# Four attention layers with exponentials on two engines: one step of VectorE's exponential and the token normalization go to GpSimd, and an unmasked pair of head groups is selected ahead

## The chip, the cores and the metric

The kernel runs on one core of a Trainium2 chip. The metric is device time in microseconds, lower is better. Before the change the median of three runs was 2004.07 us (2001.56 to 2004.95).

## The reference

Four layers work on x of 2048 tokens by 512 features, in bfloat16, with 32 heads of 16 features: A, B, A, B, with a layer norm ahead of each and a residual sum behind it. In the kernel they are layers 0, 1, 2 and 3. Layers 0 and 2 share weights, and so do 1 and 3.

```python
# A: four segments of 512 tokens, one after the other
logits = einsum('bhqd,bhkd->bhqk', qs, ks) * scale + mask     # mask is causal, inside the segment
a_dot = einsum('bhqk,bhkd->bhqd', softmax(logits), vs)
a_mem = (phi(qs) @ M) / (phi(qs) @ z + 1e-06)                  # memory of the segments before
o = g * a_mem + (1.0 - g) * a_dot                              # g = sigmoid(beta), one per head
M = M + phi(ks)^T vs;  z = z + sum(phi(ks))
# B: full attention over all 2048 tokens
p = softmax(einsum('bhqd,bhkd->bhqk', q, k) * Dh ** (-0.5))
o = einsum('bhqk,bhkd->bhqd', p, v)
```

Each layer ends with a projection by wo. The bulk of the work is the exponential of the scores: two layers of 32 heads x 2048 x 2048 unmasked, and two of 32 heads x 4 segments with the masked half of 512 x 512 left out where a whole block of it is masked.

## The kernel before

**A program written by a planner.** Python code builds the instruction lists of all engines in one pass. It keeps an estimated clock per engine (Sched, line 76) and chooses, step by step, what to issue next, so constants and estimated durations (`ns=`) decide the order of the instructions. On the chip each engine runs its own list in order, with semaphore waits where data or buffers are needed.

**Banks and units.** The scores are computed transposed, a bank at a time: 128 keys by 512 queries of one head, a 32-row matmul of K by a masked copy of Q (qm, made in line 1159, on GpSimd or on VectorE). Eight heads with one c and one parity e share a qm tile and make up groups: an A group e=0 has 12 banks and its mate 8; a B group has 16 banks for each key segment, 64 in all where all four are there. Two groups (e = 0, 1) are a pair. A unit is three banks in one half of PSUM's banks 0 to 5: TensorE fills them, one ScalarE activation of 128x1536 (line 1244) makes the exponentials, pT, and TensorE multiplies pT by V (with a column of ones for the denominators) into bank 6. Masked banks get their triangle cut by GpSimd (line 1259) in between. When a group is done, `finish` divides bank 6 by its denominators on VectorE: reciprocal (line 1312), for an A group a product with 1 - g (line 1318), and the product that makes the output tile ob (line 1324). A transposing DMA of SyncE brings ob to oT.

**Exponentials on VectorE.** `dx_pick` may take a bank of a selected B group away from ScalarE, at most one a unit. It is computed into bank 7, and VectorE evaluates the exponential by arithmetic. Line 910 evacuates the bank as a fixed-point number into dxt, KA, or QA (the names of tiles are reused as space); two banks make a chain of 1024 columns: line 936 forms z from the low half of the number, line 939 squares z, line 941 multiplies by a constant and adds another, line 943 squares again, line 945 joins the high half and writes the result dxo, which TensorE multiplies by V like any pT. Two chains (`task_dx` 0 and 1) can be under way. A group gives at most a fifth (TAKEN = 5) of its 64 banks, 12. The state is called wide once layer 0 is complete: there are then four input buffers, and one output slot more, in space that layer 0 needed.

**What sets the order.** `select` keeps a list of selected groups: it takes the next pair of A groups if its K and Q are ready, else of B groups, when at most one group is left (or two short B groups). It gives B pairs back that have not begun when an A pair of layer 2 becomes ready. Projections, layer norms, the memory of layers 0 and 2, and output projections are generator tasks; each step names what it needs, its matmuls and its VectorE time, and `background` and `bg_one` run steps as credits (CR_A in units of A groups, CR_W in wide units) and the estimated lateness of VectorE against TensorE (EARLY, DVE_LATE, DX_LATE) allow. Projections use bank 7 too. `keep_busy` adds matmuls of zeros where the planner expects TensorE to be too idle (FILL).

The layers overlap: layer 2's segments can begin once layer 1 has handed over their tokens, so four stretches of A groups of layer 2 lie between B groups of layer 1. The order in the trace is layer 0 with the first short B groups up to about 375 us; then B groups of layer 1 with the A groups of layer 2 at about 525, 771, 1017 and 1210 us; and layer 3's B groups from about 1258 us to the end.

Layer norms: for each tile of 128 tokens, statistics on VectorE (lines 511, 513), then line 538 subtracts the mean and multiplies by the reciprocal deviation, 512 columns in bfloat16, into one of two xn tiles. A transposing DMA makes xT from it.

Of the kernel before, what the change touches and what calls it, by code (L numbers as in the profile page):

```python
# [3 lines left out]
dt = mybir.dt  # L4
# [252 lines left out]
class Builder:  # L257
    NPU = 4
    WARM, WARM2 = 84, 20
    LAG_A = 2  # L260
    NDX = 4
# [12 lines left out]
    DMA_STEPS, DMA_LATE = 2, 300  # L274
# [9 lines left out]
    def alloc(self):  # L284
# [23 lines left out]
        self.qm = sb("qm", [P, 4, 512], bf)  # L308
# [10 lines left out]
        self.gout = sb("gout", [P, H], f32)  # L319
        self.M = sb("M", [P, NCH, 8, 17], f32)  # L320
# [32 lines left out]
        self.b_qm = n1("qm", 4)  # L353
# [7 lines left out]
        self.b_bet, self.b_g, self.b_gout = B("bet"), B("g"), B("gout")  # L361
        self.b_M, self.b_Mn, self.b_Mz = n1("M", 2), B("Mn"), B("Mz")
# [135 lines left out]


# [33 lines left out]
    def normalize(self, s, k, i):  # L533
        t = 4 * s + i
        n = self.ring("xn", 2)
        xn = self.xn[:, n, :]
        mean, rstd = self.lnst[:, k, i, 6:7], self.lnw[:, k, 1, i:i + 1]
        self.op("dve", lambda e: e.tensor_scalar(xn, self.x[:, t, :], mean, rstd, op0=ALU.subtract, op1=ALU.mult),
                reads=[self.b_x[t], self.b_lnst[k][i], self.b_lnw[k]], writes=[self.b_xn[n]], ns=410)
        return n, xn, self.b_xn[n]  # L540
# [213 lines left out]
    def task_out(self, L, s):  # L754
        isA = L % 2 == 0
        wo, bwo = (self.woA, self.b_woA) if isA else (self.woB, self.b_woB)
        for ti in range(4):
# [3 lines left out]
            if isA and s > 0 and ti == 0:  # L761
                for c in range(NCH):
                    yield [("dma", ("oT", L, s, c)), ("dma", ("amemT", L, s, c))], 0, 450
                    o, m = self.oT[:, 0, c, :], self.phq[:, c, :]
                    self.op("dve", (lambda o, m: lambda e: e.tensor_tensor(o, o, m, ALU.add))(o, m),
                            reads=[self.b_phq[c], self.b_oT[0][c]], writes=[self.b_oT[0][c]], ns=420)
                need.append(self.later())
# [70 lines left out]
    def dx_pick(self, items):  # L838
# [8 lines left out]
        for n, g in enumerate(self.sel):  # L847
            rest += len(g.banks) - g.pos
            if g.kind != "B" or g.total < 64 and self.near < 150 or g.shut or g.taken >= g.total // (self.TAKEN if self.wide else 6) or rest < (self.REST if self.wide else 30):
                continue  # L850
# [62 lines left out]

    def dx_close(self):
        self.dx_pairs.append((self.dx_bufs.pop(0), self.dx_build))
        self.dx_build = []

    def task_dx(self, k):
        while True:
# [3 lines left out]
            yield from self.dx_chain(k, b, ents, self.dx_free.pop(0))  # L923

    def dx_chain(self, k, b, ents, slot):
# [6 lines left out]
        out = self.dx_space("out", slot)  # L932
        z, ob = self.dx_space("z", k)[:, 0:w], out.bitcast(dt.int16)[:, 0:w]
        bt, bo, bz = self.b_dxt[b], [self.b_dxo[slot]], [self.b_dxz[k]]
# [6 lines left out]
        self.op("dve", lambda e: e.tensor_scalar(z, z, EXP_B, EXP_A, op0=ALU.mult, op1=ALU.add), reads=bz, writes=bz, ns=ns[1])  # L941
# [49 lines left out]
    def met(self, need):  # L991
# [4 lines left out]
        def ok(n):  # L996
# [6 lines left out]
            if n == "pair":  # L1003
                return len(self.dx_pairs) > 0 and len(self.dx_free) > 0
# [128 lines left out]
    def select(self, late):  # L1133
        tail = self.sel[-2:]
        if len(self.sel) > 2 and self.seqA and self.seqA[0][0].L and all(g.kind == "B" and not g.pos for g in tail) and self.met(self.group_needs(self.seqA[0][0])):
# [5 lines left out]
        while len(self.qm_free) > 1 and (len(self.sel) <= 1 or len(self.sel) == 2 and all(g.kind == "B" and g.total < 64 for g in self.sel)):  # L1141
            pair = None
            for seq in (self.seqA, self.seqB):
                if seq and self.met(self.group_needs(seq[0][0])):
                    pair = seq.pop(0)
                    break
# [4 lines left out]
            for g in pair:  # L1151
# [9 lines left out]
                self.sel.append(g)  # L1161
# [129 lines left out]
    def finish(self, g):  # L1291
# [21 lines left out]
        if g.kind == "A":  # L1313
            assert self.b_gout.last_write is not None and self.step > 2
            h = 8 * g.c + g.e
            om = bcast(self.gout[:, h:h + 1], [[0, 4], [2, 4]])
            r4 = rd.rearrange("p (t r) -> p t r", r=4)
            self.op("dve", lambda e: e.tensor_tensor(r4, r4, om, ALU.mult), reads=[br, self.b_gout], writes=[br], ns=160)  # L1318
        if g.e == 0:
            self.oi = self.ring("ob", 2)  # L1320
        oi = self.oi
# [8 lines left out]
    def run_deferred(self, now):  # L1330
        while self.deferred and (now or self.deferred[0][0] <= self.step):
            _, g, oi = self.deferred.pop(0)
            own = self.oT_owner.get((g.L % 2, g.c))
            if own is not None:
                while ("op",) + own not in self.flags:
                    self.bg_must(own)
            self.oT_owner[(g.L % 2, g.c)] = (g.L, g.qseg)
# [5 lines left out]
    def pv_taken(self, g, now, used=()):  # L1343

        for ent in [t for t in self.dxq if t[1] is g and (now or t[0] <= self.step)]:
            _, _, what, r, slot, i = ent
            if r in used:
                continue
            self.dxq.remove(ent)
            self.pv(g, what, r, self.dx_space("out", slot)[:, 512 * i:512 * i + 512], self.b_dxo[slot])  # L1350
            used = tuple(used) + (r,) if not now else ()
# [149 lines left out]
```

## Time and profile before

| what | value |
|---|---|
| median of three runs | 2004.07 us |
| the profiled execution, whole | 2004.62 us |
| its span, first to last instruction | 2002.9 us |
| mean granted TensorE clock | 0.988 |
| activations of line 1244 (three banks each) | 1413, 1712 ns each |
| banks that VectorE evacuates (line 910) | 249 + 125 + 123 = 497 |
| chains of 1024 columns, of 512 | 239, 19 |
| GpSimd's qm (line 1159), masks (line 1259) | 86.0 us, 176.6 us |
| line 1318 on VectorE | 64 times, 176 ns median |
| line 538 on VectorE | 60 times, 408 ns median |

The duration of an instruction overlaps with the next one on its engine, so durations add up to more than the time: 1413 activations of 1712 ns are 2419 us, but their union is 1912 us. What an instruction costs its engine is the spacing from start to start. An engine's busy time is the union. GpSimd's duration includes time in which it has begun and can't go on.

### The profile page before, as it was taken

Reading aid. Unit: us, or ns where it says so; the run is one execution under the profiler, and the core shown is the slowest. Engines: PE = TensorE matmul, PEld = TensorE weight load, DVE = VectorE, ACT = ScalarE, POOL = GpSimd, SP = SyncE. Lnnn points to the kernel's source line nnn. Section 1 sums busy time; section 2 is a strip of 40 time slices with the busy share of each in tenths; the row PEclk is TensorE's granted clock in tenths of the full one; section 3 lists DMA queues with packets and bytes.
Section 4 is the critical chain, followed back from the end, with each engine's and each line's share of the span. In section 5 each row is a group of like instructions: output and inputs, shape, how many; then the busy total and the mean of one; then the engine's idle time right before and its main releaser. Section 6 shows DMA issues by size and latency. Waiting matters only on the chain.

```text
span 2002.9 us, 61442 instructions
## 1 busy us (share of the span) xinstructions
PE 1721.0 (86%) x27135; PEld 890.5 (44%) x27135; DVE 1631.9 (81%) x2979; ACT 1942.2 (97%) x1456; POOL 270.5 (14%) x450
## 2 busy tenths in 40 slices
PE   7888888888878888888888888888888888888888
PEld 4444444444444444444444444444444444444443
DVE  5665555599779895899948996469999999999997
ACT  7899999999999999999999999999999999999998
POOL 3422223110220003100031004101000000000000
PEclk9999999999999999999999999999999999999999
DMA  5111111000100000000011001100000000000000
GB/s 154 33 28 18 31 28 25 4 10 15 18 10 15 5 15 20 18 15 5 15 20 18 5 17 24 20 4 7 15 5 5 5 15 5 5 5 15 5 7 12
DMA packets 100939, 34.76 MB, mean 17 GB/s; under 512 B 93504, under 2 KB 100160, under 8 KB 100672
## 3 DMA queue, kind: packets, MB, share of 16 engines
q1 hardware_dynamic: 100672, 30.83, 8.0%
q8 instruction: 212, 3.47, 0.8%
q14 instruction: 55, 0.45, 0.1%
HBM read 6.30 MB, written 2.10 MB: 4 GB/s over the span
## 4 chain that ended last, share of the span: by engine, by line
ACT 58%; issue 19%; PE 9%; DVE 6%; DMA 1%; POOL 1%; SPq 0%; ACTq 0%; DVEq 0%
ACT pT L1244 57%; PE ps L393 9%; POOL pT L1259 1%; DVE ob L1324 1%; DMA phq<-amem 1%; DVE dxt L910 1%; DVE dxo L945 1%; ACT amem L602 0%; DVE rd L1312 0%; DVE rd L1318 0%; DVE qm L1159 0%; DVE dxz L936 0%; DVE amem L691 0%; DVE KA L910 0%; DVE dxz L939 0%
## 5 line engine op out<-in xcount | busy, mean ns | idle before, releaser
L1244 ACT ACTIVATE pT<-ps 128x1536 bf16<-128x1536 f32 x1413 | 1912.4, 1712 | 43.1 <-PE ps L393 36.0
L393 PE MATMUL ps<-qm,KB 32*128 32x512 bf16 x4096 | 508.8, 386 | 192.9 <-ACT pT L1244 167.0
L393 PE MATMUL ps<-VB,pT 128*128 128x51 bf16 (+1 forms) x14396 | 578.6, 186 | 14.4 <-DVE ob L1324 6.5
L393 PEld LDWEIGHTS ps<-VB,pT 128*128 128x128 bf16 x14396 | 459.6, 96 | 294.5 <-issue 223.5
L393 PEld LDWEIGHTS ps<-qm,KB 32*128 32x128 bf16 x4096 | 130.9, 91 | 525.6 <-ACT pT L1244 487.9
L393 PE MATMUL ps<-wB,zero 128*128 128x512 bf16 x1121 | 357.9, 381 | 0.0
L1259 POOL TENSOR_SCALAR_AFFINE_SELECT pT<-pT 128x768 bf16<-128x768 bf16 (+4 forms) x320 | 176.6, 567 | 510.4 <-ACT pT L1244 509.1
L1159 POOL TENSOR_SCALAR qm<-QB,par 128x512 bf16<-128x512 bf16 x86 | 86.0, 1003 | 1117.2 <-PE ps L393 1097.3
L910 DVE TENSOR_SCALAR dxt<-ps 128x512 uint32<-128x512 f32 x249 | 170.9, 687 | 16.4 <-PE ps L393 14.5
L393 PE MATMUL ps<-VA,pT 128*128 128x51 bf16 (+1 forms) x2560 | 110.5, 190 | 34.6 <-DVE ob L1324 22.8
L393 PEld LDWEIGHTS ps<-VA,pT 128*128 128x128 bf16 x2560 | 85.0, 98 | 77.2 <-POOL pT L1259 37.0
L393 PE MATMUL ps<-qm,KA 32*128 32x128 bf16 (+2 forms) x1536 | 88.7, 260 | 21.8 <-ACT pT L1244 15.1
L393 PE MATMUL ps<-VB,dxo 128*128 128x51 bf16 (+1 forms) x1596 | 104.7, 185 | 0.3 <-DVE dxo L945 0.2
L910 DVE TENSOR_SCALAR KA<-ps 128x512 uint32<-128x512 f32 x125 | 85.7, 686 | 4.6 <-PE ps L393 3.5
L910 DVE TENSOR_SCALAR QA<-ps 128x512 uint32<-128x512 f32 x123 | 84.4, 686 | 5.5 <-PE ps L393 4.9
L939 DVE TENSOR_TENSOR dxz<-dxz 128x1024 f16<-128x1024 f16 (+1 forms) x129 | 86.9, 673 | 0.7
L943 DVE TENSOR_TENSOR dxz<-dxz 128x1024 f16<-128x1024 f16 (+1 forms) x129 | 86.5, 670 | 0.5
L939 DVE TENSOR_TENSOR VA<-VA 128x1024 f16<-128x1024 f16 (+1 forms) x129 | 86.4, 670 | 0.6
L943 DVE TENSOR_TENSOR VA<-VA 128x1024 f16<-128x1024 f16 (+1 forms) x129 | 85.4, 662 | 0.6
L393 PEld LDWEIGHTS ps<-qm,KA 32*128 32x128 bf16 x1536 | 39.1, 93 | 92.6 <-ACT pT L1244 42.3
L393 PEld LDWEIGHTS ps<-wB,zero 128*128 128x128 bf16 x1121 | 78.4, 96 | 0.0
L393 PE MATMUL ps<-xT,wA 128*128 128x512 bf16 x256 | 69.2, 388 | 1.3 <-DVE amem L691 0.4
(124 smaller groups left out, 1601.2 us busy)
## 6 DMA issues: line engine op xcount, KB each, us to landing
out_dram<-x SPq DMA_DIRECT2D x8, 256.0 KB, 2.1
x<-in_A_x_dram SPq DMA_DIRECT2D x3, 512.0 KB, 8.7
wB<-in_B_wqkv_dram SPq DMA_DIRECT2D x1, 1536.0 KB, 12.7
oT<-ob SPq DMA_TRANSPOSE x63, 2.4
xT<-xn SPq DMA_TRANSPOSE x60, 2.5
x<-in_A_x_dram SPq DMA_DIRECT2D x4, 128.0 KB, 2.2
wA<-in_A_wk_dram SPq DMA_DIRECT2D x1, 512.0 KB, 4.3
wA<-in_A_wq_dram SPq DMA_DIRECT2D x1, 512.0 KB, 5.3
```

The lines of the kernel that those rows point to most:

```text
L393: self.sc.add("pe", lambda e: e.matmul(out, lhsT, rhs, start=start, stop=stop, skip_group_check=True), reads=reads, banks=[(bank, "w", all ...
L910: self.op("dve", lambda e: e.tensor_scalar(d, o, SCALE * LOG2E * 65536, 126.0 * 65536, op0=ALU.mult, op1=ALU.add), writes=self.dx_writes(" ...
L939: self.op("dve", lambda e: e.tensor_tensor(z, z, z, ALU.mult), reads=bz, writes=bz, ns=ns[0])
L943: self.op("dve", lambda e: e.tensor_tensor(z, z, z, ALU.mult), reads=bz, writes=bz, ns=ns[0])
L945: self.op("dve", lambda e: e.scalar_tensor_tensor(ob, hi, 128.0, z, op0=ALU.mult, op1=ALU.add), reads=bt + bz, writes=self.dx_writes("out" ...
L1159: self.op(eng, (lambda m, q, col: lambda e: e.tensor_scalar(m, q, col, 0.0, op0=ALU.mult, op1=ALU.add))(m, q, col), reads=[bq, self.b_par] ...
L1244: self.sc.add("act", (lambda dst, src: lambda e: e.activation(dst, src, ACT.Exp, scale=SCALE))(dst, src), writes=self.b_pT[slot * 3 + i:sl ...
L1259: self.op("pool", (lambda blk, pat: lambda e: e.affine_select(blk, blk, pattern=pat, compare_op=ALU.is_ge, fill=0.0, base=0, channel_multi ...
L1324: self.op("dve", lambda e: e.tensor_tensor(ob, src[:, :, 0:16], rb, ALU.mult), reads=[br] + bsrc, writes=[self.b_ob[oi][g.e]], bank=bk, al ...
```

## The change

1. In `dx_chain`, the product and sum of line 941 go from VectorE to GpSimd where the state is wide and no A group is selected (`masks()`). The planner counts it as 1350 ns of GpSimd. The second square (line 943) is ordered only where the planner expects GpSimd to be done (`("done", o)`). The output slot is taken ahead of line 945 and no longer at the chain's start; there are three slots (NDX) instead of four, and one more when wide.
2. `normalize` may put line 538 on GpSimd, with no A group selected and GpSimd's estimated clock behind.
3. `select`: when wide, a full B pair is selected behind A groups, and A pairs that become ready are put in ahead of a B pair that has not begun, in place of the giving back. Six qm tiles instead of four. `dx_pick` can then take banks of that B pair while A groups run.
4. The factor 1 - g leaves `finish` (line 1318 goes). It is applied to oT, per partition, from a small tile gfm: with the sum of the memory's part in one instruction (24 times, in place of line 765's sum), and by itself in segment 0 (8 times).
5. `pv_taken` does at most one product of a taken bank a step (PV_TAKEN) in place of one a row group not in use, and `run_deferred` waits for an output projection instead of forcing it.
6. Constants of the planner: among them EARLY 400 to 200, FILL 0.58 to 0.62, CR_A 1150 to 1450, CARRY and CARRY_W 0 to 400 and 800, ALT3 2 to 1, GAP 3 to 2, PE_B and PE_A one up, DVE_LATE 1500 to 1200, DX_FIN 2500 to 9000, PAIRS2 1 to 0.

```diff
+    XN_POOL = 1
+    POOL_T = 1350
+    LOOK, PV_TAKEN = 1, 1
+    NQM = 6
-    NDX = 4
+    NDX = 3
-    EARLY = 400
-    FILL = 0.58
+    EARLY = 200
+    FILL = 0.62
-    DVE_FIN, DX_FIN = 600, 2500
+    DVE_FIN, DX_FIN = 600, 9000
-    DX_BANK, DX_LATE, BG_BANK, DVE_LATE, DVE_LATE_LOW = 500, 3000, 200, 1500, 3500
-    CR_A, CR_B, CR_W, CR_LOW, CARRY, CARRY_W, REST, NEAR, SLACK = 1150, 1500, 1700, 2600, 0, 0, 36, 30, 300
-    ALT3, ALT5, GAP, AHEAD, PE_B, PE_A, PE_LOW, LOW, PAIRS, TAKEN, PAIRS2 = 2, 4, 3, 250, 3, 2, 5, 24, 30, 5, 1
+    DX_BANK, DX_LATE, BG_BANK, DVE_LATE, DVE_LATE_LOW = 500, 3000, 200, 1200, 5000
+    CR_A, CR_B, CR_W, CR_LOW, CARRY, CARRY_W, REST, NEAR, SLACK = 1450, 1500, 1700, 2600, 400, 800, 36, 30, 300
+    ALT3, ALT5, GAP, AHEAD, PE_B, PE_A, PE_LOW, LOW, PAIRS, TAKEN, PAIRS2 = 1, 4, 2, 250, 4, 3, 5, 24, 30, 5, 0
...
+        pool = self.XN_POOL and not self.masks() and self.sc.t["pool"] < max(self.sc.t["dve"], self.sc.t["pe"])
+        self.op("pool" if pool else "dve", lambda e: e.tensor_scalar(xn, self.x[:, t, :], mean, rstd, op0=ALU.subtract, op1=ALU.mult),
...
-            if isA and s > 0 and ti == 0:
+            if isA and ti == 0:
...
+                    if s == 0:
+                        yield [("dma", ("oT", L, s, c))], 0, 360
+                        self.op("dve", (lambda o, gc: lambda e: e.tensor_scalar(o, o, gc, 0.0, op0=ALU.mult, op1=ALU.add))(o, gc),
...
+                    self.op("dve", (lambda o, m, gc: lambda e: e.scalar_tensor_tensor(o, o, gc, m, op0=ALU.mult, op1=ALU.add))(o, m, gc),
...
+    def masks(self):
+        return any(g.kind == "A" for g in self.sel)
...
-        self.op("dve", lambda e: e.tensor_scalar(z, z, EXP_B, EXP_A, op0=ALU.mult, op1=ALU.add), reads=bz, writes=bz, ns=ns[1])
-        yield [], 0, c[1]
+        o = self.op("pool" if self.POOL_T and self.wide and not self.masks() else "dve", lambda e: e.tensor_scalar(z, z, EXP_B, EXP_A, op0=ALU.mult, op1=ALU.add),
...
+        yield [("done", o)], 0, c[1]
         self.op("dve", lambda e: e.tensor_tensor(z, z, z, ALU.mult), reads=bz, writes=bz, ns=ns[0])
-        yield [], 0, c[2]
+        yield ["slot"], 0, c[2]
+        slot = self.dx_free.pop(0)
...
+            if n[0] == "done":
+                return self.bubble or self.forcing or n[1].eng == "dve" or n[1].end < max(self.sc.t["dve"], self.sc.t["pe"]) + 60
...
+            look = self.LOOK and self.wide
+            at = next((i for i, g in enumerate(self.sel) if g.kind == "B" and g.e == 0 and not g.pos), len(self.sel)) if look else len(self.sel)
+            few = at <= 1 or not look and at == 2 and all(g.kind == "B" and g.total < 64 for g in self.sel)
+            short = look and len(self.sel) == 2 and all(g.kind == "B" and g.total < 64 for g in self.sel)
+            if self.seqA and (few or short) and self.met(self.group_needs(self.seqA[0][0])):
+                pair = self.seqA.pop(0)
...
+            elif self.seqB and at == len(self.sel) and (few or short or look and self.seqB[0][0].total == 64 and all(g.kind == "A" for g in self.sel)) and self.met(self.group_needs(self.seqB[0][0])):
+                pair = self.seqB.pop(0)
...
-                self.sel.append(g)
+                self.sel.insert(at + i, g)
...
-        if g.kind == "A":
...
-            self.op("dve", lambda e: e.tensor_tensor(r4, r4, om, ALU.mult), reads=[br, self.b_gout], writes=[br], ns=160)
```

More of the change, by code (lines that the diff above doesn't have):

```diff
@@ L1150, in select @@
                 return
-            for g in pair:
+            for i, g in enumerate(pair):
                 g.qm = self.qm_free.pop(0)
@@ L1343, in pv_taken @@
     def pv_taken(self, g, now, used=()):
+        n = 0
         for ent in [t for t in self.dxq if t[1] is g and (now or t[0] <= self.step)]:
             _, _, what, r, slot, i = ent
-            if r in used:
-                continue
+            if not now and n == self.PV_TAKEN:
+                break
+            n += 1
             self.dxq.remove(ent)
             self.pv(g, what, r, self.dx_space("out", slot)[:, 512 * i:512 * i + 512], self.b_dxo[slot])
-            used = tuple(used) + (r,) if not now else ()
             self.dx_use[slot] -= 1
```

72 lines of the change are left out of this document (44 added, 28 removed).

## The prediction

> **What bounds the kernel now.** I read the page's busy shares, slices and chain first, then the busy time by stretch, then the groups by shape, and last the order of time of VectorE and GpSimd around single GpSimd instructions.
>
> ```profile
> span 2002.9 us, 61442 instructions
> PE 1721.0 (86%) x27135; PEld 890.5 (44%) x27135; DVE 1631.9 (81%) x2979; ACT 1942.2 (97%) x1456; POOL 270.5 (14%) x450
> DVE  5665555599779895899948996469999999999997
> ACT  7899999999999999999999999999999999999998
> ACT 58%; issue 19%; PE 9%; DVE 6%; DMA 1%; POOL 1%; SPq 0%; ACTq 0%; DVEq 0%
> ```
>
> ScalarE is busy 97% of the span and heads the chain: the exponentials are the bound. Only 60 us of it are idle, 25 of them in the first 100 us by the table of stretches. So the kernel gets faster in one main way: VectorE must take more score banks away from ScalarE. The DVE row says where it could. In the long unmasked stretches it is full; ahead of them, and in dips in the middle, it is not.
>
> ```profile
> 1350.00:1950.00 600.00, 515.70 (x8464) 259.11 (x8460) 588.71 (x950) 599.84 (x448) 29.68 (x26) 1.00 0.03 7
> ```
>
> ```profile
> 525.00:565.00 40.00, 32.18 (x581) 18.15 (x576) 20.24 (x49) 38.41 (x30) 19.65 (x36) 1.00 0.23 28
> 771.00:811.00 40.00, 32.57 (x537) 17.21 (x537) 22.34 (x51) 38.73 (x30) 20.67 (x37) 0.96 0.14 28
> 1017.00:1057.00 40.00, 32.33 (x555) 18.15 (x550) 21.50 (x48) 38.62 (x31) 18.12 (x33) 0.96 0.18 28
> ```
>
> The columns after the length are PE, PEld, DVE, ACT, POOL, clock and DMA. In the last 600 us ScalarE and VectorE are both full: 448 activations of three banks, 1.339 us each start to start, so **a bank is worth 0.446 us of ScalarE**. VectorE evacuates 248 banks there (line 910). The three 40 us stretches are the masked segments of layer 2: ScalarE still sets the pace, VectorE is half idle (56 us idle in all), and it takes practically no bank in them (0.09 us of line 910 in the first two).
>
> **What a bank costs VectorE.** From the order of time at 1890 us, start to start: line 936 0.60, line 939 0.60, line 941 0.335, line 943 0.60, line 945 1.245, and two evacuations (line 910) of 0.605. A pair of banks is 4.59 us, a bank 2.29 us.
>
> **Part 1, line 941 to GpSimd.** The groups by shape:
>
> ```profile
> L1159 POOL TENSOR_SCALAR qm<-QB,par 128x512 bf16<-128x512 bf16 x86 | 86.0, 1003 | 1117.2 <-PE ps L393 1097.3 <-DVE x L777 15.5 <-DVE QB L420 4.4
> L941 DVE TENSOR_SCALAR dxz<-dxz 128x1024 f16<-128x1024 f16 x122 | 52.3, 429 | 0.7
> L941 DVE TENSOR_SCALAR VA<-VA 128x1024 f16<-128x1024 f16 x117 | 49.2, 421 | 0.5
> ```
>
> VectorE loses about 230 of its 258 chains' line 941 (those outside the masked windows, counted in 50 us stretches): 230 x 0.335 = 77 us gross. Refilled with banks, that is 77 / 2.29 = 33 banks, 33 x 0.446 = 15 us of ScalarE. GpSimd has the time: undisturbed, 512 elements take it 0.695 us (the shortest rows of line 1159), and the mask rows of line 1259 grow by 0.88 ns an element (313 ns at 128, 876 ns at 768), so 1024 take about 1.15 us, 230 of them 265 us. The other chain covers that latency; if both chains wait on GpSimd, VectorE stands still, since its queue is in order and the second square (943) heads it.
>
> But the two engines are not independent. GpSimd's 128x512 instruction takes 0.695 us alone and 1.003 us in the mean. Around 1535 us:
>
> ```profile
> 1535.39 0.71 DVE L939 TENSOR_TENSOR dxz<-dxz 128x1024 f16<-128x1024 f16 x1
> 1536.02 1.10 DVE L936 TENSOR_SCALAR VA<-QA 128x1024 f16<-128x1024 uint16 x1
> 1537.05 0.41 DVE L941 TENSOR_SCALAR dxz<-dxz 128x1024 f16<-128x1024 f16 x1
> 1537.38 0.68 DVE L910 TENSOR_SCALAR dxt<-ps 128x512 uint32<-128x512 f32 x1
> ```
>
> ```profile
> 1535.38 1.20 POOL L1159 TENSOR_SCALAR qm<-QB,par 128x512 bf16<-128x512 bf16 x1 [21.94 <-PE ps L393]
> ```
>
> GpSimd starts beside line 939 and seems to get nothing until 939 ends at 1536.10; it ends at 1536.58. Line 936, which takes 0.69 elsewhere, takes 1.10: it stood 0.41 us. Around 1137 us GpSimd loses instead: it runs 2.13 us across lines 936 and 945 and ends 0.48 us after 945 does. Lines 936, 939, 941, 943 and 945 all show such +0.4 us; line 910, which reads PSUM, never does. **So a GpSimd read of 512 elements holds something for 0.42 to 0.48 us that every step of the chain needs and the evacuation does not.** The Trainium skill, page "SBUF — State Buffer", section "Who interferes with whom", calls it a port pair that is locked for a whole instruction, and the loser blocks; its page "Perfetto Trace Analysis" warns that offloading between these two engines might not help. The rows above agree with the lock. By that rule alone part 1 would gain nothing, which is the third and fourth case below.
>
> What does it cost here? Of 28 GpSimd instructions from 1328 us on, 4 stopped VectorE by 0.41 to 0.42 us and one by 0.06: 62 ns in the mean, because mostly GpSimd loses and then gets its turn under an evacuation of 0.605 us. At 1024 elements the hold is about 0.85 us, and an evacuation no longer covers it. Lower bound: twice 62, 124 ns. Upper bound: (24 x 0.25 + 4 x 0.84) / 28 = 334 ns if each turn under an evacuation leaves 0.25 us to wait, and to 0.95 us if VectorE comes to line 943 before GpSimd had its turn. I take 200 ns, between the first two and nearer to the row. Net 135 ns x 230 = 31 us of VectorE, 13.5 banks, **-6 us** (from -15 with no blocking to a loss).
>
> **Part 2, an unmasked pair selected ahead.** In the three masked stretches VectorE would now find banks to take. 56 us idle / 2.29 = 24 banks, x 0.446 = 11 us. These banks count against the same cap of 12 a group, the groups already give 10 (248 banks in 24 groups), and bank 7 is shared with the projections there; I count two thirds: **-7 us** (0 to -11).
>
> **Part 3, the gate leaves the group's end.** Line 1318 goes, 64 times; reciprocal to product falls from about 0.55 to 0.28 us, 64 x 0.276 = 17.7 us of shorter turns of the accumulator. TensorE waits 67 us in all for line 1324, but ScalarE is idle only 10 us between 100 and 350 us and about 3 in each masked window: **-3 us** (0 to -8). Added: 24 sums become scaled sums (0.69 by half of line 945, against 0.496: +4.6 us) and 8 new scalings (0.41 each, line 538's row: 3.3 us), in stretches where VectorE has room. Nothing on the path; if that room is filled, 8 us / 2.29 x 0.446, 1.5 us.
>
> **Part 4, normalizing on GpSimd.** Some 28 of the 60 tiles fall in unmasked stretches: 28 x (0.335 - 0.06) = 8 us of VectorE, 3 banks, **-2 us** (0 to -2). Each feeds a transposing DMA on SyncE's queue, up to 2 us later; behind it in that queue are only transposes, and projections have slack in unmasked stretches.
>
> **Part 5, the planner's constants.** They change the order, not the work: more background per masked unit (CR_A, PE_A), credit carried over, picks in each step (ALT3). ScalarE's 35 idle us outside the start-up bound what they can give. More dummy matmuls (FILL) buy clock that is already 0.988. I take **-3 us** (-8 to +8). Three output slots for four cost nothing as long as slots are taken only ahead of line 945, as they now are; else chains wait.
>
> **Sum.** -6 -7 -3 -2 -3 = -21 us. The profiled execution took 2004.62 us (span 2002.9, 1.7 around it); that is 0.5 above the median of the three, so no correction: **1983 us**.
>
> **Rivals.**
> - *The port is nearly free* (GpSimd's turns fall under evacuations) and the pair ahead fills the masked stretches: -15 -11 -6 -2 -5 = -39, 1965. For it: 24 of 28 rows. Against: the hold is twice as long. Chance 0.16.
> - *The pair ahead does nothing*: what it gives early is missing from the cap later, and part 1 is small: -3 -3 -2 -3 = -11, 1993. For it: ten of twelve already used. Chance 0.14.
> - *Break-even at the port*: 334 ns of block for 335 saved, and the planner's orders lose 4 to 10 us: 2000 to 2008. Chance 0.10.
> - *The port decides against it (slower).* VectorE is full in 1100 us of span; the block falls straight on it, and its evacuations hold bank 7 and so TensorE and ScalarE. Each nanosecond of block above 335 costs 230 ns: at 500 ns, 165 x 230 = +38, less 15 of the other parts: 2028. It decides from about 400 ns on. For it: at contested ends of instructions GpSimd lost about 12 times of 17, so VectorE may arrive at line 943 first and then stand for the whole 0.85. A planner that counts the freed 0.335 as room and fills it makes this worse. Against: line 910 comes twice a pair. Chance 0.22.
>
> **Numbers.** The forecast (1970 to 1996) has 0.38; with the first two rivals, faster by over 0.2% has 0.68, within 0.2% (about what a measurement can tell) 0.10, slower 0.22. The range, 1955 to 2032, reaches over the port-free case and up to a block of some 520 ns.
>
> **What would show it.** Line 941 as a GpSimd row of about 230, 1.15 us at its shortest and 1.4 to 1.6 in the mean; lines 939, 943, 945, 936 longer by 0.4 to 0.9 in some tens of cases; VectorE evacuations up from 497 to about 540, activations down from 1413 to about 1399; line 910 present in the masked stretches; the reciprocal followed at once by line 1324. Wrong: fewer evacuations, ScalarE idle in the last 600 us, or idle time of VectorE ahead of line 943 released by GpSimd.

## The result, and the profile after

The change makes the kernel slower: 2070.1 us median (2067.6 to 2071.26, four runs) against 2002.87 us, a ratio of 1.0332 with a 95% interval of 1.0315 to 1.0349, **+67 us**. The profiled execution took 2067.6 us, its span 2065.7. The forecast was 1983. Lines 910, 936, 939, 941, 943, 945 and 538 of before are lines 930, 959, 962, 964, 967, 971 and 552 now; the activation is line 1287.

The page of the kernel after: busy shares, the same two slice rows as before with the clock's, and the chain.

```profile
span 2065.7 us, 61943 instructions
PE 1808.5 (88%) x27327; PEld 918.2 (44%) x27327; DVE 1708.7 (83%) x2786; ACT 1939.7 (94%) x1443; POOL 726.2 (35%) x727
DVE  5655553799988998999997676479999999999997
ACT  7889999999999998999999999999999999999998
PEclk9999999999999998999999999999999999999999
DVE 52%; PE 17%; ACT 16%; issue 10%; POOL 4%; DMA 1%; SPq 0%; ACTq 0%; DVEq 0%; POOLq 0%
```

The head of the chain has changed hands: ScalarE had 58% of it and has 16, VectorE had 6% and has 52. ScalarE is as busy as before, but for 63 us more of span. Now the groups of GpSimd by shape:

```profile
L964 POOL TENSOR_SCALAR dxz<-dxz 128x1024 f16<-128x1024 f16 x116 | 176.6, 1522 | 393.3 <-DVE dxz L962 390.3 <-PE ps L400 2.4
L964 POOL TENSOR_SCALAR VA<-VA 128x1024 f16<-128x1024 f16 x117 | 167.8, 1434 | 370.0 <-DVE VA L962 366.8 <-PE ps L400 2.4
L552 POOL TENSOR_SCALAR xn<-x,lnst,lnw 128x512 bf16<-128x512 bf16 x36 | 84.8, 2358 | 95.7 <-DVE lnw L543 77.9 <-DMA xT<-xn 17.1
```

The work moved as forecast: some 230 products and sums of 1024 columns at 1.43 to 1.52 us; VectorE's evacuations rose from 497 to 538, activations fell from 1413 to 1400 (forecast: 540 and 1399). The time went the other way. The longest waits say where:

```profile
PEld ps L400 <- ACT pT L1287: 317.0, 683, 1.5
ACT pT L1287 <- PE ps L400: 97.0, 157, 2.7
...
PEld ps L400 <- DVE dxt L930: 68.2, 105, 2.4
```

Columns are us in total, times, and the longest. TensorE waited 530.8 us for ScalarE ahead of a weight load and waits 317 now; ScalarE's wait for TensorE went from 36 to 97 us, most of the time lost; and TensorE's wait for VectorE's evacuation of bank 7 into dxt went from 7.7 to 68.2 us. VectorE is late, TensorE, which runs its list in order, stands behind bank 7, and ScalarE starves.

The stretch with layer 3's long groups, 600 us of it (columns as in the prediction):

```profile
1420.00:2020.00 600.00, 535.19 (x8239) 260.91 (x8237) 583.85 (x827) 578.35 (x427) 236.13 (x151) 0.98 0.04 7
```

ScalarE had 599.84 us and 448 activations there; it has 578.35 and 427. VectorE is as full as it was.

### The profile page after: what moved, and what is told of

Its sections match the earlier page's. It is cut to its first block, busy times and chain, and to the rows that moved or that the text cites. A ratio compares the mean times of both kernels' runs of the same rounds, so it can differ in the third digit from the quotient of the medians.

```text
span 2065.7 us, 61943 instructions
## 1 busy us (share of the span) xinstructions
PE 1808.5 (88%) x27327; PEld 918.2 (44%) x27327; DVE 1708.7 (83%) x2786; ACT 1939.7 (94%) x1443; POOL 726.2 (35%) x727
## 4 chain that ended last, share of the span: by engine, by line
DVE 52%; PE 17%; ACT 16%; issue 10%; POOL 4%; DMA 1%; SPq 0%; ACTq 0%; DVEq 0%; POOLq 0%
PE ps L400 17%; ACT pT L1287 16%; DVE dxo L971 9%; DVE dxt L930 6%; DVE dxz L959 4%; DVE VA L959 3%; DVE QA L930 3%; DVE dxz L962 3%; DVE VA L971 3%; DVE VA L962 3%; DVE KA L930 3%; DVE dxz L967 3%; DVE VA L967 3%; DVE ob L1363 2%; POOL xn L552 2%
## 5 line engine op out<-in xcount | busy, mean ns | idle before, releaser
L1287 ACT ACTIVATE pT<-ps 128x1536 bf16<-128x1536 f32 x1400 | 1910.1, 1500 | 104.9 <-PE ps L400 97.0
L400 PE MATMUL ps<-qm,KB 32*128 32x512 bf16 x4096 | 572.0, 392 | 139.9 <-ACT pT L1287 54.8
L400 PE MATMUL ps<-VB,pT 128*128 128x51 bf16 (+1 forms) x14232 | 579.8, 187 | 24.2 <-DVE ob L1363 15.5
L400 PE MATMUL ps<-wB,zero 128*128 128x512 bf16 x1313 | 423.9, 389 | 0.0
L1302 POOL TENSOR_SCALAR_AFFINE_SELECT pT<-pT 128x768 bf16<-128x768 bf16 (+4 forms) x320 | 190.7, 611 | 402.4 <-ACT pT L1287 401.1
L964 POOL TENSOR_SCALAR dxz<-dxz 128x1024 f16<-128x1024 f16 (+1 forms) x124 | 185.4, 1495 | 413.6 <-DVE dxz L962 410.5
L964 POOL TENSOR_SCALAR VA<-VA 128x1024 f16<-128x1024 f16 (+1 forms) x123 | 175.6, 1428 | 386.2 <-DVE VA L962 382.9
L930 DVE TENSOR_SCALAR dxt<-ps 128x512 uint32<-128x512 f32 x271 | 185.2, 683 | 18.2 <-PE ps L400 15.0
L400 PEld LDWEIGHTS ps<-VA,pT 128*128 128x128 bf16 x2560 | 84.7, 97 | 84.5 <-POOL pT L1302 43.9
L552 POOL TENSOR_SCALAR xn<-x,lnst,lnw 128x512 bf16<-128x512 bf16 x36 | 84.8, 2358 | 95.7 <-DVE lnw L543 77.9
L962 DVE TENSOR_TENSOR dxz<-dxz 128x1024 f16<-128x1024 f16 (+1 forms) x140 | 102.1, 729 | 0.6
L967 DVE TENSOR_TENSOR VA<-VA 128x1024 f16<-128x1024 f16 (+1 forms) x139 | 97.6, 702 | 4.8 <-POOL VA L964 4.6
L962 DVE TENSOR_TENSOR VA<-VA 128x1024 f16<-128x1024 f16 (+1 forms) x139 | 100.9, 726 | 0.4
L967 DVE TENSOR_TENSOR dxz<-dxz 128x1024 f16<-128x1024 f16 (+1 forms) x140 | 96.2, 687 | 3.9 <-POOL dxz L964 3.6
L971 DVE SCALAR_TENSOR_TENSOR dxo<-dxt,dxz 128x1024 int16<-128x1024 uint16 (+1 forms) x70 | 92.3, 1319 | 0.3
```

The costliest lines, as they stand in the source:

```text
L400: self.sc.add("pe", lambda e: e.matmul(out, lhsT, rhs, start=start, stop=stop, skip_group_check=True), reads=reads, banks=[(bank, "w", all ...
L552: self.op("pool" if pool else "dve", lambda e: e.tensor_scalar(xn, self.x[:, t, :], mean, rstd, op0=ALU.subtract, op1=ALU.mult), reads=[se ...
L930: self.op("dve", lambda e: e.tensor_scalar(d, o, SCALE * LOG2E * 65536, 126.0 * 65536, op0=ALU.mult, op1=ALU.add), writes=self.dx_writes(" ...
L964: o = self.op("pool" if self.POOL_T and self.wide and not self.masks() else "dve", lambda e: e.tensor_scalar(z, z, EXP_B, EXP_A, op0=ALU.m ...
L971: self.op("dve", lambda e: e.scalar_tensor_tensor(ob, hi, 128.0, z, op0=ALU.mult, op1=ALU.add), reads=bt + bz, writes=self.dx_writes("out" ...
L1287: self.sc.add("act", (lambda dst, src: lambda e: e.activation(dst, src, ACT.Exp, scale=SCALE))(dst, src), writes=self.b_pT[slot * 3 + i:sl ...
```

## The experiments

Times are medians. "Before" in the runs beside them was 2001.87 to 2003.06.

### What the product and sum on GpSimd cost

**Back on VectorE** (planned there, too):

```diff
-    POOL_T = 1350
+    POOL_T = 0
```

> The kernel after, with the product and sum of the chain back on VectorE and planned there; all else of the change stays. Theory (the port's lock takes back what the move frees, and the planner has filled the freed time with 41 more banks): the lock's 70 us of longer VectorE instructions go, evacuations fall from 538 to about 510, time 1985 to 2010. Rival (the planner's new constants, the pair ahead or the normalization on GpSimd cost the time): over 2050.

Measured: 2028.8 us, ratio 1.0131 [1.0112, 1.0151]; 41 us come back, 27 stay. The time fell between the two theories: the rest of the change costs as well. The evacuations went from 538 to 520, so the product's move had brought 18 of the 41 additional banks.

**GpSimd writes only** (the product and sum are left out), with the order of the kernel after kept:

```diff
-        o = self.op("pool" if ... else "dve", lambda e: e.tensor_scalar(z, z, EXP_B, EXP_A, ...
+        fn = (lambda e: e.memset(z, 1.5)) if pool else (lambda e: e.tensor_scalar(z, z, EXP_B, EXP_A, op0=ALU.mult, op1=ALU.add))
```

> The kernel after in its own order, but GpSimd writes a constant over z instead of the product and sum, so it reads nothing there; the exponentials of those chains are left out of the result. Theory (a GpSimd read locks what VectorE's two-input and fast steps need): the longer squares, joins and first steps mostly vanish, ScalarE's idle time ahead of the activations falls from 105 us to under 60, time 2000 to 2025. Rival (the order itself is bad, or the extra engine crossing): over 2050 with the same order.

Measured: 2008.77 us, ratio 1.0044 [1.0029, 1.006]. The instruction on GpSimd is still there, 0.946 us at its shortest against 1.044, and so are the order, the waits, and the normalization. Without the read 61 of the 67 us are gone. Part of this is the shorter wait (0.98 us in the mean against 1.46), but in the kernel after VectorE had waited for line 964 only some 8 us in all, and it waits 9 us here. The same stretch (its profiled execution was one of its longer ones, 2016.68):

```profile
1370.00:1970.00 600.00, 542.18 (x8619) 264.85 (x8616) 586.35 (x871) 599.37 (x447) 148.27 (x160) 1.00 0.03 8
```

ScalarE is full again, with VectorE doing 261 banks beside it in place of 247.

What the read does is seen in the order of time of the kernel after, VectorE first, then GpSimd:

```profile
1875.27 0.68 DVE L930 TENSOR_SCALAR QA<-ps 128x512 uint32<-128x512 f32 x1
1875.87 1.67 DVE L971 SCALAR_TENSOR_TENSOR dxo<-dxt,dxz 128x1024 int16<-128x1024 uint16 x1
1877.57 0.69 DVE L930 TENSOR_SCALAR dxt<-ps 128x512 uint32<-128x512 f32 x1
```

```profile
1875.42 1.04 POOL L964 TENSOR_SCALAR VA<-VA 128x1024 f16<-128x1024 f16 x1 [2.42 <-DVE VA L962]
```

GpSimd gets its turn beside the evacuation, as the prediction assumed, and runs its shortest time; line 971, begun 0.45 us after it, takes 1.67 in place of 1.22. And where line 971 comes first:

```profile
1870.28 0.68 DVE L962 TENSOR_TENSOR dxz<-dxz 128x1024 f16<-128x1024 f16 x1
1870.88 1.22 DVE L971 SCALAR_TENSOR_TENSOR VA<-QA,VA 128x1024 int16<-128x1024 uint16 x1
1872.02 0.68 DVE L930 TENSOR_SCALAR KA<-ps 128x512 uint32<-128x512 f32 x1
1872.62 0.93 DVE L959 TENSOR_SCALAR VA<-dxt 128x1024 f16<-128x1024 uint16 x1
```

```profile
1871.05 1.96 POOL L964 TENSOR_SCALAR dxz<-dxz 128x1024 f16<-128x1024 f16 x1 [3.91 <-DVE dxz L962]
```

GpSimd stands until line 971 ends at 1872.10, and line 959 pays 0.24 us. Counted over the whole kernel: of VectorE's instructions that begin while GpSimd is at such an instruction of 1024 columns, and overlap it by 0.1 us or more, these took over 0.1 us longer than their usual time in the kernel before (the last column is the run in which GpSimd only writes; squares, joins and first steps are those of 1024 columns):

| VectorE's instruction | beside product and sum | beside the write alone |
|---|---|---|
| join (971), two inputs | 45 of 48, mean +0.46 us | 0 of 42 |
| squares (962, 967), two inputs | 36 of 36, mean +0.48 us | 0 of 42 |
| first step (959), one input | 89 of 89, mean +0.22 us | 11 of 11, mean +0.30 us |
| evacuation of 512 columns (930), from PSUM | 0 of 101 | 0 of 26 |

The Trainium skill, page "SBUF — State Buffer", section "Who interferes with whom", says that whoever issues first gets the shared pair for the whole instruction while the other blocks, and that a VectorE instruction with two inputs contends with a GpSimd instruction that reads SBUF, not with one that only writes it. The counts agree with it on who stops whom, and so do the two rows above, in both directions; for how much of an instruction the pair is held they do not settle.

Added over the whole span, VectorE's instructions that run over 100 ns beyond the median of their group (same operation, tiles and shape) in the kernel before exceed it by 25.1 us before, 104.9 after, 28.3 with the product back, 43.9 with the write alone.

**Charged to both.** The planner books 345 ns of VectorE for each instruction that GpSimd does:

```diff
+        if o.eng == "pool":
+            self.sc.t["dve"] += self.LOCK
```

> The kernel after, but the planner books 345 ns of VectorE for each product and sum on GpSimd, as if it still cost VectorE that much; on the chip GpSimd does it. Theory (refill): the plan takes about 500 banks instead of 538, VectorE is no longer overfilled, time 2000 to 2030. Rival (each lock stall hits TensorE and ScalarE however the plan is filled): over 2045. Second rival (constants): over 2045 too.

Measured: 2037.15 us, ratio 1.0178 [1.0155, 1.02], 33 us under the kernel after, 8 over the one with the product on VectorE. It fell between the two theories: 33 of the 41 us come back when the plan counts VectorE's time as taken. That undoes two things at once, the additional banks (521 evacuations in place of 538) and an order laid out for a faster VectorE than the chip has; the run does not part them. 8 us stay, with the instruction still on GpSimd.

**Alone in the kernel before:**

```diff
-        self.op("dve", lambda e: e.tensor_scalar(z, z, EXP_B, EXP_A, op0=ALU.mult, op1=ALU.add), reads=bz, writes=bz, ns=ns[1])
-        yield [], 0, c[1]
+        pool = self.wide and not any(g.kind == "A" for g in self.sel)
+        o = self.op("pool" if pool else "dve", ..., ns=1350 if pool else ns[1])
+        yield [("done", o)], 0, c[1]
```

> The kernel before with only the product and sum on GpSimd (booked 1350 ns there, the second square ordered behind it as in the change); no other part. Theory (lock and refill): slower, 2030 to 2070, with evacuations up by 15 to 40 and first steps, squares and joins longer by 50 us or more. Rival (constants or other parts cost the time): 1995 to 2010.

Measured: 2059.91 us, ratio 1.0291 [1.027, 1.0311]. The excess of VectorE's long instructions is 86.7 us (25.1 before), so **a product and sum on GpSimd blocks VectorE for (86.7 - 25.1) / 258 = 0.24 us**. (Counting only instructions that begin beside a product, it is 0.22 us here and 0.27 in the kernel after.) The evacuations are only 507, 10 more than before, where 15 to 40 were expected.

The long stretch of layer 3, 600 us in each kernel, shows how the loss comes about there. Share is VectorE's part of all banks; a bank's time is 600 / (evacuations + 3 x activations) by the starts inside.

| kernel | evacuations, activations | share | VectorE busy us a pair | us a bank |
|---|---|---|---|---|
| before | 247, 447 | 15.6% | 4.77 | 0.378 |
| after | 250, 426 | 16.4% | 4.67 | 0.393 |
| before with product on GpSimd | 247, 419 | 16.4% | 4.71 | 0.399 |
| after, charged | 243, 441 | 15.5% | 4.59 | 0.383 |
| after, product on VectorE | 244, 445 | 15.5% | 4.79 | 0.380 |
| after, GpSimd only writes | 261, 446 | 16.3% | 4.49 | 0.375 |

The planner believes that a pair has become 0.335 us (7%) cheaper, and gives VectorE 5% more of the banks (15.6 to 16.4%). On the chip a pair has become 1 to 2% cheaper. VectorE was full, so the time per bank must rise by about the difference, 3 to 4%; it rose by 4.0% in the kernel after and by 5.6% with the product's move alone. Where the read is taken away a pair is 0.27 us cheaper, and the same refill pays: 0.375. With the plan charged the share is that of before and VectorE has time to spare (558 of 600 us busy), yet a bank takes 0.383: what is left there are stalls.

The refill is a matter of place, not of number. Nearly all of the new banks lie in layer 3, counted here from the 2850th bank on (1272 us in the kernel before). With the move alone VectorE takes 284 there in place of 273, is busy 697 us in place of 677, and the layer lasts 34 us longer; in the kernel after, against the one with the product back, it is 285 for 270, 694 for 676 us, and 21 us. But 20 and 17 us of the loss come ahead of layer 3, where VectorE takes 1 bank fewer and 3 more. More banks cannot be the cause there. With the move alone TensorE's weight loads wait 25 us for evacuations of taken banks in that part in place of 7, and ScalarE waits 28 us for TensorE in place of 16: the blocked VectorE comes late to bank 7 there, too. That is 12 of the 20 us; what the rest is was not shown.

### The normalization

The kernel before, with this part alone, once planned anew and once in its own order (booked as if on VectorE):

```diff
+        pool = not any(g.kind == "A" for g in self.sel) and self.sc.t["pool"] < max(self.sc.t["dve"], self.sc.t["pe"])
-        self.op("dve", lambda e: e.tensor_scalar(xn, ...), ..., ns=410)
+        self.op("pool" if pool else "dve", lambda e: e.tensor_scalar(xn, ...), ..., ns=900 if pool else 410)
```

> The kernel before with the normalization alone on GpSimd, under the change's condition. Prediction's step: 2 us faster. By the 2.06 us that a tile takes there at its shortest (0.42 on VectorE): first projections of a segment up to 8 us later and the port held for longer; 2003 to 2015.

> The kernel before in its own order, with the normalization of unmasked stretches on GpSimd, booked in the planner as if on VectorE, so that all else stands where it stood. The prediction's step: 2 us faster. If the 13 us of the normalization alone come from 2.06 us a tile and the port: 2008 to 2016. If they come from the new order: 2000 to 2005.

Measured: 2016.95 us (1.0067 [1.0052, 1.0082]) and 2012.63 us (1.0042 [1.0027, 1.0057]). The instruction itself, in the second kernel:

```profile
L538 POOL TENSOR_SCALAR xn<-x,lnst,lnw 128x512 bf16<-128x512 bf16 x41 | 96.7, 2362 | 327.3 <-DVE lnw L530 312.7 <-DMA xT<-xn 14.5
```

2.36 us in the mean and 2.07 at its shortest, where VectorE takes 0.42 and where GpSimd's line 1159, of the same shape with one per-partition factor, takes 0.69. It hardly blocks VectorE: the excess of long instructions is 26.5 us there, 25.1 before, and of the chain's first steps, squares and joins of 1024 columns that begin beside it 5 of 41 are over 0.1 us longer, where beside a product and sum 170 of 173 are. The page's rule cited above, as it reads, does not tell the two apart; the measurement decides. So the 8 us are not the blocked port. That they are later transposes and projections is likely, but not shown.

With both moves undone the kernel after stays slow:

```diff
-    XN_POOL = 1
-    POOL_T = 1350
+    XN_POOL = 0
+    POOL_T = 0
```

> The kernel after with both moves to GpSimd undone (product and sum, normalization); the pair ahead, the gate's new place and the constants stay. In the run with only the product and sum back, 27 us over the kernel before were left. Theory A (normalization on GpSimd at 2.1 to 2.4 us a tile delays projections and holds the port): 2005 to 2017. Theory B (constants or the pair ahead cost it): 2022 to 2032.

Measured: 2033.11 us (1.0151 [1.0136, 1.0166]), 4 us over the kernel that normalizes on GpSimd. Theory A fell: in this order the move costs nothing that can be told.

### The pair ahead

Each of these starts from the kernel with both moves undone (2033.11 us).

```diff
-    LOOK, PV_TAKEN = 1, 1
+    LOOK, PV_TAKEN = 0, 1
```

> The kernel after with both moves to GpSimd undone and without the pair ahead; new constants, gate, slots stay. Theory (banks taken in the masked stretches hold up VectorE's other work there, TensorE waits for it, its clock falls to 0.8 to 0.9 and ScalarE idles): 2003 to 2015, with masked stretches at full clock. Rival (constants, gate, slots): 2025 to 2035.

```diff
-        if self.low or self.near < self.PAIRS ...
+        if self.masks() and items[0][0].kind == "A" or self.low or self.near < self.PAIRS ...
```

> As the kernel after with both moves undone, pair ahead on, but no bank is taken in a unit that begins with an A group's bank. Theory (the picks in masked units are what costs): 2005 to 2017. Rival (the selection order itself, A pairs put in ahead of B pairs): 2025 or more.

Measured: 2008.71 us (1.0028 [1.0014, 1.0042]) and 2014.82 us (1.0058 [1.0038, 1.0079]). The pair ahead costs 24 us, and 18 of them are the banks taken in masked units, the very thing from which the prediction expected 7 us. In the kernel with both moves undone, the masked stretches look like this:

```profile
575.00:600.00 25.00, 20.40 (x321) 10.42 (x322) 22.32 (x40) 21.67 (x17) 12.96 (x22) 0.89 0.08 17
600.00:625.00 25.00, 17.88 (x321) 10.13 (x313) 22.96 (x45) 21.04 (x16) 18.73 (x23) 0.91 0.10 13
775.00:800.00 25.00, 16.45 (x229) 8.56 (x229) 20.32 (x29) 15.28 (x13) 7.99 (x9) 0.80 0.11 23
850.00:875.00 25.00, 18.93 (x290) 9.58 (x289) 22.50 (x38) 18.75 (x14) 12.66 (x21) 0.80 0.13 12
```

VectorE's idle time is filled (20 to 23 of 25 us), and ScalarE loses up to 9.7 of 25 us. Among TensorE's waits there is that for line 1363, the product that ends a group: its weight loads wait 50 us for it in all, 37 without the pair ahead, and the longest such wait, near 780 us (the third window), is 7.3 us (2.5 in the kernel before). VectorE, TensorE and ScalarE there, in the kernel with both moves undone:

```profile
784.12 1.87 DVE L971 SCALAR_TENSOR_TENSOR dxo<-dxt,dxz 128x1024 int16<-128x1024 uint16 x1
788.30 0.25 DVE L1355 RECIPROCAL rd<-ps 128x16 f32<-128x16 f32 x1
788.59 0.42 DVE L1363 TENSOR_TENSOR ob<-ps,rd 128x256 bf16<-128x256 f32 x1
```

```profile
789.07 1.39 PE L400 MATMUL ps<-VA,pT 128*128 128x51 bf16 x28 [6.99 <-DVE ob L1363]
```

```profile
789.62 1.45 ACT L1287 ACTIVATE pT<-ps 128x1536 bf16<-128x1536 f32 x1 [6.64 <-PE ps L400]
```

From 775.41 to 787.70 VectorE does nothing but 14 steps of chains of taken banks (one of them is shown); the two short steps that free bank 6 stand behind them in its list, and TensorE and ScalarE wait 7 us. The idle time of VectorE in masked stretches was not all spare: the ends of groups have to be prompt there, and elsewhere the evacuations: from 840 to 900 us TensorE's weight loads wait 6.0 us for evacuations of taken banks and 1.4 us for line 1363. The granted clock falls to 0.80 to 0.91 in these windows. Whether it is a cause of its own was tried with more matmuls of zeros:

```diff
-    FILL = 0.62
+    FILL = 0.85
```

> As the kernel after with both moves undone, with FILL 0.85 in place of 0.62: more matmuls of zeros where the planner sees TensorE idle. If the dips of the granted clock are a cause of their own: clock up from 0.978 to 0.985 or more, time 2010 to 2025. If they only follow TensorE's stalls: clock and time within 5 us of 2033, or slower, as the added matmuls stand ahead of others.

Measured: 2043.43 us (1.0198 [1.0176, 1.0221]): the mean clock rises from 0.978 to 0.984, the time by 10 us. The higher clock did not bring the time back; what the added matmuls cost by themselves the run does not part from it. Without the pair ahead the clock is 0.986 with no change to the matmuls of zeros, so it is likely, but not shown, that the dips only follow the stalls.

### The constants

The planner's constants of before, first with the pair ahead, then without it (shortened; the other constants of the change go back, too):

```diff
-    EARLY = 200
-    FILL = 0.62
+    EARLY = 400
+    FILL = 0.58
...
-    CR_A, CR_B, CR_W, CR_LOW, CARRY, CARRY_W, REST, NEAR, SLACK = 1450, 1500, 1700, 2600, 400, 800, 36, 30, 300
+    CR_A, CR_B, CR_W, CR_LOW, CARRY, CARRY_W, REST, NEAR, SLACK = 1150, 1500, 1700, 2600, 0, 0, 36, 30, 300
```

> As the run with both moves undone, and the planner's constants (EARLY, FILL, CR_A, CARRY, ALT3, GAP, PE_A, PE_B and the others, not the numbers of tiles and slots) are those of before. Left of the change: pair ahead, gate, slot taken late, one product of a taken bank a step. Theory (constants cost the rest): 1988 to 2006. Rival (the pair ahead spends the cap of 12 early and leaves VectorE idle later): 2012 to 2030.

> As the run with the old constants, and also without the pair ahead. Left: gate, slot taken late, one product of a taken bank a step, three output slots. By the prediction's step on the gate 3 us below before: 1996 to 2004. If the pair ahead costs, this one is 10 us or more under the run with the pair ahead; if it gives 7 us as predicted, it is 7 over it.

Measured: 2041.62 us (1.0184 [1.0163, 1.0205]) with the pair ahead and 2026.95 us (1.0118 [1.0103, 1.0133]) without it. So the theory of these two runs fell: against the kernels with the new constants (2033.11 and 2008.71 us) the old ones cost 8.5 us with the pair ahead and 18 without. Nearly all of it is one gap early on, here in ScalarE's order of time in the second kernel:

```profile
116.61 1.45 ACT L1287 ACTIVATE pT<-ps 128x1536 bf16<-128x1536 f32 x1
120.20 0.60 ACT L425 ACTIVATE VB<-ps 128x512 bf16<-128x512 f32 x1 [2.14 <-PE ps L400]
123.88 0.60 ACT L425 ACTIVATE VB<-ps 128x512 bf16<-128x512 f32 x1 [3.08 <-PE ps L400]
127.51 0.60 ACT L425 ACTIVATE KB<-ps 128x512 bf16<-128x512 f32 x1 [3.02 <-PE ps L400]
```

From 118 to 141 us ScalarE has no bank to exponentiate and only evacuates projections; in the kernel before, with the same constants, it exponentiates without a gap there. The first 400 banks are done 23 us later than in the kernel before, and the whole span is only 24 us longer. With the pair ahead and the old constants it is 25 us at that point and 38 at the end; with the pair ahead and the new ones 0 and 27. So the new constants help by not having this gap. Which of them does it, and which other part of the change makes it necessary, was not tried. The pair ahead costs here, too: 15 us, where it is 24 with the new constants.

### The gate, and how much any new order moves the time

```diff
-            self.op("dve", lambda e: e.tensor_tensor(r4, r4, om, ALU.mult), reads=[br, self.b_gout], writes=[br], ns=160)
+            fake = Op("dve", 0, None)
...
```

> The kernel before in its own order, without the 64 products of line 1318 (the factor 1 - g is left out of the result). The prediction's step: 3 us faster, 0 to 8. Rival (the accumulator's turns are hidden): within 1 us.

Measured: 1998.21 us, ratio 0.9969 [0.9952, 0.9985]: about 5 to 6 us faster, in the range of the prediction's step (the factor 1 - g is left out there; the planner books its time as before, so that the order stays). A complete kernel that has the factor in V's column of ones:

```diff
+                src = bcast(self.gout[:, 0:1], [[0, 8], [1, H]])
+                self.op("dve", lambda e: e.tensor_copy(va, src), reads=[bd], writes=[b for l in self.b_VA for b in l])
...
-            self.op("dve", lambda e: e.tensor_tensor(r4, r4, om, ALU.mult), reads=[br, self.b_gout], writes=[br], ns=160)
```

> The kernel before in its own order, complete: the column of ones of layers 0 and 2's V holds 1 + exp(beta), so that the reciprocal of the denominator already has the factor 1 - g, line 1318 goes, and the memory's factor becomes exp(beta). If the shorter end of a masked group is worth what the run without the product showed: 1995 to 2000.

Measured: 2000.8 us, ratio 0.9989 [0.9975, 1.0004]: the best complete version tried, but not told apart from the kernel before.

Two kernels do all but the same work as before (496 evacuations for 497) in a slightly different order, by a constant moved a little (SLACK 300 to 330; a booked 850 to 900):

> The kernel before with one planner constant moved by a tenth (SLACK 300 to 330); the same work in another order. If the planner's order is robust: within 4 us of before. If before sits on a lucky order: 8 to 30 us slower, and then differences of that size between re-planned kernels say nothing of the edited part.

> The kernel before with one booked credit moved (the layer norm's statistics step costs 900 in place of 850); the same work in another order. Robust order: within 4 us of before. Lucky order: 8 to 30 us slower.

Measured: 2006.63 us (1.0017 [1.0007, 1.0027]) and 2004.87 us (1.0013 [1.0, 1.0026]). These two new orders by themselves move the time by 0.1 to 0.2%, 3 to 4 us. So the differences of 4 to 6 us above may be luck of the planner; those of 8 us and more are less likely to be, though two small moves do not bound what a larger one can do.

## Why the prediction was wrong

By single steps from the kernel after to the kernel before: charging the planner for the blocked time 33 us, the product back on VectorE 8, the normalization back -4, no pair ahead 24, the rest (constants, gate, slots, products of taken banks) 6; together 67. The sizes hold for this order of steps: alone in the kernel before the product's move costs 58 us, not 41.

- **Part 1, the step that failed first.** "I take 200 ns, between the first two and nearer to the row. Net 135 ns x 230 = 31 us of VectorE, 13.5 banks, **-6 us**". The block was near: 0.24 us alone, up to 0.27 in the kernel after, inside 0.124 to 0.334, though its row misled: beside line 1159's instruction in the kernel before 9 of 31 steps of the chain (first steps, squares and joins) ran longer, beside the product 170 of 173. GpSimd's durations were right (1.04 us at the shortest, 1.43 to 1.52 in the mean). Even the banks came, 18 in the kernel after and 10 alone. What failed is the step from banks to time. The sum let the chip's freed time pay for them, wherever it is freed. The planner sets them by the 335 ns that it believes free, nearly all of them in layer 3, where VectorE had no room and a pair had become only 1 to 2% cheaper: VectorE's busy time rose there by 17 to 20 us, and with it the time. And the blocked VectorE comes late to bank 7 also where it takes no more banks, and TensorE and ScalarE wait for it; for this the sum had no term. The fourth rival had this path and even the sentence on the planner, but put the deciding point at "about 400 ns on"; at 0.24 us the part alone costs 58 us. Its price, 230 ns for each nanosecond above 335, is what the runs refute.
- **Part 2** was wrong in sign: -7 forecast, +24 measured. "56 us idle / 2.29 = 24 banks" took idle time of VectorE for spare time. The banks came (523 evacuations with the pair ahead, 503 without, both moves undone), but their steps stand ahead of the ends of groups, as the rows near 780 us show. The second rival guessed that the cap of 12 would take later what the pair ahead gives early; 20 banks more in all speak against that.
- **Part 3** was right in size where it could be isolated (-5 to -6 for -3, 0 to -8), but in a complete kernel not told apart from nothing.
- **Part 4** priced VectorE's side alone, "28 x (0.335 - 0.06) = 8 us of VectorE". The block was no larger than its 0.06 us (1.4 us of excess over 41 tiles), but the delay of each tile, which it put at nothing, was not free: 2.36 us on GpSimd for 0.42. It costs 8 to 14 us alone, and nothing that can be told in the changed order.
- **Part 5** was right in direction: the new constants help the new structure by 8.5 and 18 us (-3 forecast), but by a gap near 120 us that the kernel before does not have, so this is no gain over it.
- **The range** ended at 2032 because it allowed one block of some 520 ns and no loss by the pair ahead. Most of the signs listed to show the steps right came true: evacuations, activations, GpSimd's rows, some tens of longer steps of the chain (line 959's, at 0.22 us in the mean, shorter than the 0.4 to 0.9 forecast). They tell that the work moved, not that it paid. Of the three signs listed against, ScalarE idle in the last 600 us (22 us in place of 0.2) was the one that carried the time; idle time of VectorE ahead of line 967 (943 before), released by GpSimd, came too, but small (8 us).

Open stays what the rest of the cost of the product's move ahead of layer 3 is, what the 8 us of the normalization on GpSimd are made of, and the last 6 us (constants, gate in its new place, slots, and the products of taken banks), which are near what a new order moved.

## What to carry to other kernels

Where a static plan fills an engine to the brim, moving a step off it is worth what the chip gives back, less what the plan has already spent; book the moved step's hindrance on the old engine too, or the plan can turn a small gain into a loss. More work taken over is no sign of time saved: here the banks came as forecast and the time went the other way. Idle time of an engine that others wait for is not all spare time: before filling it, look at which short steps of it are on somebody's path there. And look for the nearest row by operands, not by shape alone, before pricing an instruction on another engine.

## What the runs showed of the hardware that was not expected

- On GpSimd a 128x512 bf16 instruction takes 0.69 us at its shortest with one per-partition operand and an immediate (multiply, add), and 2.06 us with two per-partition operands (subtract the mean, multiply by the reciprocal deviation); 128x1024 in f16 with two immediates takes 1.044 us. The operators differ too, so which of the two makes it slow was not parted.
- Beside the product and sum, which reads, every square and all but 3 of 48 joins of VectorE ran longer, by 0.46 to 0.48 us in the mean; beside one of nearly the same length that only writes (0.946 us), none of 84 did. The first step of the chain, with one input, ran longer beside both (0.22 and 0.30 us). In the same order 61 us of the time went with the read.
- A longer GpSimd instruction isn't a worse neighbour: beside the 2.06 us normalization 5 of 41 steps of the chain ran longer, beside the 1.04 us product 170 of 173.
